# One accumulation bank for a unit's split and plain products, scaled in place, with new lists for the whole order

## The chip, the cores and the metric

The kernel runs on one core of one Trainium2 chip. The metric is the device time of one execution in microseconds; the figure given is the median of several runs. An engine is called by the short name that the profile uses: PE (TensorE, matmuls), PEld (its weight loads), DVE (VectorE), ACT (ScalarE), POOL (GpSimd), SP (SyncE, which issues most DMAs).

## The reference

The input x has 4 batches of 12416 rows of 128 channels. An attention block with 32 inducing rows comes first, then a gated feed-forward layer with RMS norm, of width 1536. Both in fp32.

```python
def mab(q, kv):
    s = scale * (q @ kv.transpose(0, 2, 1))
    s = s - s.max(-1, keepdims=True)
    a = np.exp(s)
    a /= a.sum(-1, keepdims=True) + 1e-09
    return a @ kv
h = mab(I, x)
x = mab(x, h)                       # (4 * 12416, 128)

rms = np.sqrt(np.mean(x * x, axis=-1, keepdims=True) + 1e-06)
xn = x / rms * rms_g
g = xn @ w_gate                     # 128 -> 1536
silu = g * (1.0 / (1.0 + np.exp(-g)))
out = (silu * (xn @ w_val)) @ w_out # 1536 -> 128
```

## The kernel before

**Tiling.** The rows of a batch are cut into 7 sets, and these into 25 units of 512 columns (the sixth set's are 480, the last one's 256): 100 units in all. Rows stand in columns, so a unit is a moving operand of 128 x 512. The width 1536 is cut into 12 pieces of 128; one piece of one unit is a block, 1200 in all. The list `sorts` gives each block one of three kinds.

**One block.** `gate` (L720) and `value` (L748) are one matmul each, with operands rounded to fp32r in two halves so that the sum is nearly fp32. `silu` (L730) takes the gate from PSUM on ACT. `times_value` (L762) multiplies it by the value on DVE. What follows depends on the kind:

- P, plain: the factor u is fp32 in SBUF, and `project_plain` multiplies it by the fp32 third matrix (L818, tile `wo`). The profile shows each of these fp32 products as two matmul instructions.
- S, split on DVE: u stays in PSUM. `high` (L775, ACT) rounds it to fp32r, scaled by about -2^-12; `low` (L781, DVE) makes the rest; `project_two` issues two fp32r matmuls (L806, L807); `add_in_place` (L826, POOL) adds the two parts; `project_third` issues a third fp32r matmul (L818, through `project`).
- D, split on POOL: u is in SBUF, `high` is at L772, `low_of_u` (L788) is on POOL and `high_down` (L794) on ACT; then as S.

**One unit.** The two matmuls of all its split blocks sum in one PSUM bank, `ups`. The thirds and the plain products sum in another, `acc`. `scale_up` (L850, ACT) reads `ups`, multiplies by 1 + 2^-12 and writes it to a buffer o in SBUF, four column groups apart. `finish` (L859, DVE) adds `acc` to it, `turn_out` (L865, DVE) transposes it in 32 x 32 blocks in place, `store` (L880) issues four DMAs.

**Order.** Everything is written out by hand, as lists of letters that were found beforehand: `program` is the order in which instructions are emitted, so the order on each engine; `.` in it is a step of attention, of its norm or of the preparation of weights, taken from `micros` by the list `taken`. `banks` gives the PSUM bank (of 8) for each matmul result, `holders` the buffer (of 19, 9 in pool `up` and 10 in three spare tiles of x) for u, high and low, `outputs` the buffer o, `sorts` the kinds, and `picks` which of the blocks that wait for a step is taken next. An engine takes its instructions in that order and waits at each until its operands are there.

**Around it.** The first 42 us load x, the weights and the first attention scores (`first`); after that the block loop runs to the end, with the attention of the next batch between the blocks. `rooms` runs between the two: the tiles of x of sets 2 to 4 of the first batch become the 10 further buffers.

Of the kernel before, what the change touches and what calls it, by code (L numbers as in the profile page):

```python
# [18 lines left out]
P = 128  # L19
# [4 lines left out]
def kernel(  # L24
# [40 lines left out]
    RING, HELD, SILU = 4, 9, 3  # L65
# [17 lines left out]
    psum = pool("psum", 1, space=PSUM)  # L83
    pall = psum.tile([P, 8, 512], F32, name="gv")
# [9 lines left out]
    def load_rows(b, s):  # L94

        n = per[s]
        t = xnat[b, s] = xnp.tile([P, 16 if b and n > 4 else n, C], F32, name=f"xn{s % 2 if b and n > 4 else s}")
# [592 lines left out]

    blocks, kinds = [], []
# [7 lines left out]
    def unit_of(b, u):  # L699
        if (b, u) not in at_unit:  # L700
            s, q = units[u]
            at_unit[b, u] = {"T": per2[s] * m, "a": moving.pop((b, u)), "left": NJ, "q": 0, "acc": None,
                             "k": sum(kind != "P" for kind, one in zip(kinds, blocks) if one[:2] == (b, u)), "o": None,
                             "ups": None}
# [92 lines left out]
    def project_two():  # L797
# [4 lines left out]
        if one["ups"] is None:  # L802
            one["ups"] = bank()
        to = one["ups"][:, 0:T]
# [6 lines left out]
    def project(n, lhsT, rhs, step2):  # L811
# [3 lines left out]
        if one["acc"] is None:  # L815
            one["acc"] = bank()
        to = one["acc"][:, 0:T]
        nc.tensor.matmul(to.rearrange("p (n h) -> p h n", h=2) if step2 else to, lhsT, rhs,  # L818
                         start=one["left"] == NJ, stop=one["left"] == 1)
# [18 lines left out]
    leaving = {name: 0 for name in "EFTO"}  # L838

    def next_unit(name):  # L840
        leaving[name] += 1
        return flat[leaving[name] - 1]

    def scale_up():
# [3 lines left out]
        T, o = one["T"], output(F32)  # L848
        one["o"] = o
# [11 lines left out]
    def turn_out():  # L861
        b, u = next_unit("T")
        one = unit_of(b, u)
        o, T = one["o"], one["T"]
# [393 lines left out]
    def seams():  # L1258
# [13 lines left out]
        5674130256741352764156216710562160121607267012750671527162067125701527061352701372301273016276370142374017436107  # L1272
        5461701375601735764301674317642376476324736426173214672670321071507125625625730261325620463042603435423046754672
        6571574124615247601207502765127520730717157312014520712054051402460524124361406470341720123014073145207145205162
        4076176230451603542360267402340264706402613067507602716510250673501637521352614563175416571674605740534715702545
        3457042563253265431275126142745265124560124607164701640316370347147057304132041201372013720317603270307256042750
        4756027457256347203174063021462176270675246510461307635063450634573460543604265230541265026504265026316241321643
        1064370613041320741327342735407234507234657403254130421502401325140275130732713621762170617301612506031041234610
        4621046513052135720175237120372130276215601670416415074560743514305436543215362160524062534217541646314735673157
        3561746147560274265462502530726546253601460362013460724104270371274205402507215724175061045614061306531405310463  # L1280
        5013674034130461204372104672503725074604365073047654304716046074107160721504712670235072130536725603505237062407
        2314760162062746015412574251346547516421541257642576072605210572153701357127034152342375276132436236724632174260
        7540152406524150621504361053606250125726507650216745012475627452743564527342654736024670261720742160726034704320
        1472014721542015430174301574231654215634251467354216352615236025301253012765320532154725347254712563174217637523
        0752370635767540372103120437204312072430730145703175601314341703641706327102751301341735407364103410543265123614
        2351425312634175725647256172010457015472134270321026701630513620712605763476237062046267210473623561561453612546
        3210523025043570145370641763120547163047305173501630763120750674561027475467045074507245626034013453165034150326
        4520132435743051217230723165016371043651306704754053640356435270342704175027517251427507164721453264534516342164
        5320164532405127451723407312403612753123512561726532756127032160342560324053246302542164321024052472014725041275
        4327031240370173104731643143072641362013562150613570615263174521621452643256416312654036254720764065205621562756  # L1290
        0461043103560401403507471054615042704627160734102374130415021704170527054761045260123646504615304673106351670515
        6725120513657106723017346123461762167341527647362746502364576215367425762156246276570647274635074067450367513541
        3657426517365127605360130232046352162146574051760415704761350735705327537210570673160752635725473427635274152645
        3273157425073215023576031706527106241065476140173546703573061362013651036013243162015714251640542016204310546154
        3103601765732053210642367412702173273407417520715231603573156743061471567051725417627452617425143610742642604276
        0124051264701256140
    """
    workers = """
        20120201201201020120122201201201201201211210210201020120110120120
    """  # L1300
    outputs = """
        10101010101010101010101010101010101010101010101010101010101010101010101010101010101010101010101010101010
    """
    holders = """
        abcdefghibcaedfghbicjkadelmfghnobcidepqarsfgbhidjkaeclmpnfoqrsgjhbidklaecpnfgdombrqsjihpagoecdfbknilmpghrqfsjlmc
        pkinobrsadqjhpkgfelmnoqcjrspbliadnmjkoqsglhrfejpaodnqbscriekjapmlnsqogkrbfpjhsaecokqrmdilnopgskmhqbcjrefolmnipqs
        ajdgchmkfepoirnbgqlsrpmckjfoqglnpsmibkohadprelsjmcgfnkbqolpiahdrjemsqfrcgbhnoiljepkqmrsdnloaqjifrcgpmsonblkqejrp
        hsgialnfqpojmkdsrlnqcpombeijsplqhfdagknromqepijchalskdgfbrmepqjnhgaifcokjpbrlqgeinosmdrlajpqhskmnrcfbloqmjidesag
        frklcjpqnosmhbdrlgiejkafdqpcbrmelonsfgcqjidpkhablroqenmfgicdjshaoedcinpqlgbjkhsdiorfbhgemnaqocspfjkrigbhdlmasncq
        pfedjorgbsnkclqmhefirjabposknlqemdrgibfhpoqscajnlmfhkrpecidjnbgqosljmafkdpnrqcoskihgbpefcadjlmrhosapndqkgehpjmin  # L1310
        obflrqdspkcmjnqholgaesbfkpdolhminqfjrskcpogmljdfnrqbpcaoskjhgiqmlpnefodqrmknlpcsmijknabolpshgjeidbfocgnkhqrplmjs
        oaifehgcnbdkpqclhrgfdesmjnrofkqilpgsrobkdjqlmhcnseljamrpqknfoiglspmcoqjkldhrsnpelabjmokqngircjfdhblsemqpnokjgamq
        rdlipejfmscpqonklhmgsaberjocpikmlpdsrhefqngobaljpikdmhcqsrleonfagbmpjreqolciknmpsqholfjgbakderichfsnmqopaljbrkcf
        moglhiaedbrjckqegdpsnlfrjiedkqmoaghcpsnrfblmikendagojlqhcfbmpiarsnlgckmfdhqbpoidejnaqkhipdgerbasohjlgmqienpfkrcs
        adhjnglmbpsqofekrjpidgscbljqnhepkafomgisqrnbplkcohjmfsrgkpaqbeoijdlsgnmqrfeokabpjnmlcgqhafdibeopgsrklnjcqmobkgln
        hsqdpriomajlkceshnpbofiarqsmndgejklobipnhcsgldefmraqchbjkopaslmnqirohjgdqbpmeknfsalrcidjfqokegplsdjmrknbsphcgljr
        mqasifnpeokljdhcgfrqmsolnpbekjromialsfnqpkgrjmondqlhscpnkrmbefiaojsqglkdphnmrclskoerigapjnrfbkdhlosqnmpkrsjelgpi
        acnhfjrmlpoqkdnsjbremgqkfjapdhnrifmlcesqjkbgophnrmjceoslpnadkqimofjgnbshdrlcminjoeafbkqdgpschmnjofrpdksblqamrige
        jnchpoblkqsfdagmjirnpohecqslkrpbmjdfnloqaskighmoeqcbsjrpnlagqmdikshofnejcabrlgqpdmkohirnbsldfaqjcpmkoriegsqlknjp
        ofdbshemrlqpncsgoaibklpmejshnqorkcjbplnfksqomjrdgapnqkoemicrlphjqbgnmorsfakjploqcsdnipebghorfcqksmlpjonradbcqfse  # L1320
# [240 lines left out]
```

## Time and profile before

| | |
|---|---|
| Median of 3 runs | 1467.7 us (1467.61 to 1468.09) |
| Span of the profiled execution | 1467.1 us |
| What lies around the span | 0.6 us from the span to the median |
| Instructions in the profile | 25864 |
| HBM | 53.95 MB read, 27.00 MB written |

The profile is one execution. Its span goes from the first to the last instruction. "Busy" is the time in which an engine has an instruction running; matmuls are pipelined, so the length of one record (0.38 us for 512 columns) is not what it takes of PE; the distance between starts is. A group's line gives its count, the busy time and the mean of one in ns, then the idle time of the engine just before such instructions and what ended it.

### The profile page before, as it was taken

The page shows a single profiled execution, that of the slowest core. Times are in us where ns is not written, and L with a number is a line of the kernel's source. Part 1 is how long each engine was busy: PE and PEld are TensorE (multiplying, and loading weights), DVE is VectorE, ACT ScalarE, POOL GpSimd, SP SyncE. Part 2 cuts the span into 40 slices and gives each one's busy share as a digit, 9 for nine tenths or more (in the row PEclk, how much of TensorE's full clock was granted, in tenths as well). Part 3 has the DMA queues.
Part 4 walks back from the last instruction along what each step waited for, and adds up shares of the span by engine and source line. Part 5 has one row for each costly group of instructions (what it writes and reads, how often), then busy time and mean ns, then how long its engine had stood idle before and what let it go on. Part 6 is the DMA issues. An engine that isn't in the chain of part 4 may idle for free.

```text
span 1467.1 us, 25864 instructions
## 1 busy us (share of the span) xinstructions
PE 1460.2 (100%) x7293; PEld 1111.8 (76%) x7293; DVE 1423.3 (97%) x2476; ACT 1300.0 (89%) x2586; POOL 1353.0 (92%) x1193
## 2 busy tenths in 40 slices
PE   9999999999999999999999999999999999999998
PEld 7556777877777777786777778777778778788787
DVE  6999999999999999999999999999999999999998
ACT  6798899889988989988999899888998999899987
POOL 2578998999999999899999999799999999999998
PEclk9999999999999999999999999999999999999999
DMA  7656224445654222635554132355123111222121
GB/s 282 137 99 119 58 49 92 103 107 99 118 88 99 38 44 44 141 84 105 110 101 82 26 73 43 63 119 127 34 62 70 33 37 39 43 42 38 36 45 33
DMA packets 391904, 116.02 MB, mean 79 GB/s; under 512 B 365648, under 2 KB 371280, under 8 KB 389200
## 3 DMA queue, kind: packets, MB, share of 16 engines
q1 hardware_dynamic: 391168, 114.28, 37.7%
q8 instruction: 58, 0.95, 0.3%
q14 instruction: 86, 0.70, 0.2%
q10 hardware_dynamic: 592, 0.08, 0.0%
HBM read 53.95 MB, written 27.00 MB: 55 GB/s over the span
## 4 chain that ended last, share of the span: by engine, by line
PE 99%; DVE 0%; DMA 0%; ACT 0%; issue 0%; DVEq 0%
PE gv L818 33%; PE gv L720 17%; PE gv L748 17%; PE gv L806 12%; PE gv L807 12%; PE gv L327 3%; PE gv L380 1%; PE gv L945 1%; PE gv L574 1%; PE gv L989 0%; PE gv L468 0%; PE gv L158 0%; PE gv L490 0%; DMA ind<-in_inducing_dram 0%; PE gv L567 0%; PE gv L1099 0%
## 5 line engine op out<-in xcount | busy, mean ns | idle before, releaser
L730 ACT ACTIVATE silu<-gv 128x512 f32<-128x512 f32 (+2 forms) x1200 | 678.1, 591 | 89.4 <-PE gv L720 67.4
L826 POOL TENSOR_TENSOR xn<-xn,xn 128x512 fp32r<-128x512 f32 (+2 forms) x363 | 453.0, 1259 | 23.4 <-PE gv L807 14.5
L720 PE MATMUL gv<-a,sg 128*128 128x512 f32 (+2 forms) x1188 | 463.5, 415 | 0.1
L748 PE MATMUL gv<-a,sv 128*128 128x512 f32 (+2 forms) x1188 | 460.9, 415 | 0.0
L762 DVE TENSOR_TENSOR gv<-silu,gv 128x512 f32<-128x512 f32 (+2 forms) x649 | 427.1, 673 | 6.5 <-ACT silu L730 2.2
L775 ACT ACTIVATE xn<-gv 128x512 fp32r<-128x512 f32 (+2 forms) x602 | 353.1, 594 | 25.8 <-DVE gv L762 20.5
L818 PE MATMUL gv<-u,wo 128*128 128x512 f32 (+2 forms) x742 | 364.1, 576 | 0.0
L762 DVE TENSOR_TENSOR u<-silu,gv 128x512 f32<-128x512 f32 (+2 forms) x551 | 352.3, 654 | 7.8 <-PE gv L748 3.7
L826 POOL TENSOR_TENSOR u<-xn,u 128x512 fp32r<-128x512 f32 (+2 forms) x239 | 298.3, 1257 | 5.6 <-PE gv L807 4.1
L720 PEld LDWEIGHTS gv<-a,sg 128*128 128x128 f32 x1188 | 223.9, 189 | 86.8 <-issue 21.5
L748 PEld LDWEIGHTS gv<-a,sv 128*128 128x128 f32 x1188 | 223.8, 189 | 80.6 <-issue 23.0
L781 DVE SCALAR_TENSOR_TENSOR xn<-xn,gv 128x512 fp32r<-128x512 f32 (+2 forms) x410 | 268.9, 662 | 4.7 <-ACT xn L775 2.7
L826 POOL TENSOR_TENSOR xn<-xn 128x512 fp32r<-128x512 f32 (+2 forms) x170 | 211.4, 1250 | 11.4 <-PE gv L807 10.3
L806 PE MATMUL gv<-xn,xn 128*128 128x512 f32 (+2 forms) x450 | 177.4, 394 | 0.0
L818 PEld LDWEIGHTS gv<-u,wo 128*128 128x128 f32 x742 | 139.1, 190 | 29.7 <-issue 14.2
L788 POOL TENSOR_TENSOR xn<-u,xn 128x512 fp32r<-128x512 f32 (+2 forms) x123 | 152.3, 1243 | 6.8 <-ACT xn L772 5.5
L781 DVE SCALAR_TENSOR_TENSOR u<-xn,gv 128x512 fp32r<-128x512 f32 (+2 forms) x192 | 125.8, 660 | 1.2 <-ACT xn L775 0.9
L818 PE MATMUL gv<-xn,xn 128*128 128x512 f32 (+2 forms) x299 | 117.3, 398 | 0.0
L806 PE MATMUL gv<-xn,more 128*128 128x512 f32 (+2 forms) x302 | 116.0, 385 | 0.0
L794 ACT ACTIVATE xn<-xn 128x512 fp32r<-128x512 f32 (+2 forms) x170 | 105.6, 623 | 8.2 <-POOL xn L788 4.0
L807 PE MATMUL gv<-xn,xn 128*128 128x512 f32 (+2 forms) x299 | 111.6, 373 | 0.0
L772 ACT ACTIVATE xn<-u 128x512 fp32r<-128x512 f32 (+2 forms) x170 | 104.9, 621 | 3.9 <-DVE u L762 1.7
(233 smaller groups left out, 2049.8 us busy)
## 6 DMA issues: line engine op xcount, KB each, us to landing
out_dram<-o SPq DMA_DIRECT2D x320, 64.0 KB, 2.0
xT<-in_x_dram SPq DMA_DIRECT2D x60, 256.0 KB, 4.1
xn<-in_x_dram SPq DMA_DIRECT2D x60, 256.0 KB, 5.0
a<-hi SPq DMA_DIRECT2D x152, 64.0 KB, 2.0
a<-lo SPq DMA_DIRECT2D x152, 64.0 KB, 2.0
xn<-in_x_dram SPq DMA_DIRECT2D x5, 1024.0 KB, 9.6
xn<-w SPq DMA_DIRECT2D x18, 256.0 KB, 4.6
out_dram<-o SPq DMA_DIRECT2D x64, 60.0 KB, 2.1
```

Of the source, the lines that this page charges most:

```text
L720: nc.tensor.matmul(g[:, 0:T], stacks[b][0][:, ts(j, P)], halves_in_turn(one["a"][:, 0:T]), start=True, stop=True)
L730: nc.scalar.activation(sl[:, 0:T], gates.pop(n)[:, 0:T], AF.Silu)
L748: nc.tensor.matmul(v[:, 0:T], stacks[b][1][:, ts(j, P)], halves_in_turn(one["a"][:, 0:T]), start=True, stop=True)
L762: nc.vector.tensor_tensor(out=to, in0=sl[:, 0:T], in1=v[:, 0:T], op=ALU.mult)
L775: nc.scalar.activation(hi, t["u"], AF.Copy, scale=-(1.0 - 2.0 ** -13) * 2.0 ** -12)
L781: nc.vector.scalar_tensor_tensor(out=t["lo"], in0=t["hi"].bitcast(F32), scalar=4096.0, in1=t["u"], op0=ALU.mult, op1=ALU.add)
L788: nc.gpsimd.tensor_tensor(out=t["lo"], in0=t["u"], in1=t["hi"].bitcast(F32), op=ALU.subtract)
L794: nc.scalar.activation(t["hi"], t["hi"].bitcast(F32), AF.Copy, scale=-(2.0 ** -12))
L806: nc.tensor.matmul(to, weight_of(0, j), halves_in_turn(t["hi"]), start=not one["q"], stop=False)
L807: nc.tensor.matmul(to, weight_of(1, j), halves_in_turn(t["lo"]), start=False, stop=last)
L818: nc.tensor.matmul(to.rearrange("p (n h) -> p h n", h=2) if step2 else to, lhsT, rhs, start=one["left"] == NJ, stop=one["left"] == 1)
L826: nc.gpsimd.tensor_tensor(out=t["lo"], in0=t["hi"].bitcast(F32), in1=t["lo"].bitcast(F32), op=ALU.add)
```

## The change

In all units but the first four (`APART = 4`), `project_two` sums into the same bank as the thirds and plain products, `acc`. When a unit's last second matmul is done, `scale_up` multiplies that bank by 1 + 2^-12 in place, PSUM to PSUM, and only then the thirds and plain products of the unit are added to it (`start` is false for them). `finish` is left out for these units. `turn_out` transposes from PSUM, through the strided view that `finish` and `scale_up` used, into o. E, T and O, which took units in turn, now take them by `picks`.

The 10 further buffers are tiles of a pool of their own, `ring`, each with a name, in the room of another pool, `xlp`, that holds sets 2 to 4 of the first batch and is closed in `rooms`; before they were slices of three tiles.

All lists are new. The counts that can be read from them:

| list | before | after |
|---|---|---|
| `sorts`: P, S, D | 371, 649, 180 | 338, 718, 144 |
| `program`: F | 100 | 4 |
| `program`: h, q, d, r each | 829 | 862 |
| `program`: l, n and e, p | 649, 180, 371 | 718, 144, 338 |
| `program`: g, s, v, m, and E, T, O | 1200 each, and 100 each | the same |
| `banks` | 2707 | 2611 |
| steps in `taken` | 879 | 879, the same ones in another order |

The lists of the first 42 us (`BANKS`, `WORKERS`, `OUTPUTS`, `ORDER`) are unchanged.

```diff
+    late = {"ctx": ctx.enter_context(ExitStack())}
+    late["x"] = late["ctx"].enter_context(tc.tile_pool(name="xlp", bufs=1))
...
     def rooms():
         kws["first"] = xnp.tile([P, half + NK, C], F32R, name=f"xn{full - 1}")
-        rings = [xnp.tile([P, RING * 512], F32R, name=f"xn{full - 4 + n}") for n in range(3)]
-        for n in range(3 * RING - 2):
-            kws[HELD + n] = rings[n // RING][:, ts(n % RING, 512)]
-        kws["last"] = rings[2][:, 2 * 512:4 * 512].rearrange("p (k c) -> p k c", c=C)
+        late["ctx"].close()
+        late["ring"] = pool("ring", 1)
+        kws["last"] = late["ring"].tile([P, 8, C], F32R, name="last")
...
     def room(kind=F32R):
         n = factors.pop(0)
-        return up.tile([P, 512], kind, name="u", tag=f"u{n}") if n < HELD else kws[n]
+        return (up if n < HELD else late["ring"]).tile([P, 512], kind, name="u", tag=f"u{n}")
...
     def project_two():
...
-        if one["ups"] is None:
-            one["ups"] = bank()
-        to = one["ups"][:, 0:T]
+        name = "ups" if one["apart"] else "acc"
+        if one[name] is None:
+            one[name] = bank()
+        to = one[name][:, 0:T]
...
     def project(n, lhsT, rhs, step2):
...
+        assert one["apart"] or one["scaled"]
         to = one["acc"][:, 0:T]
         nc.tensor.matmul(to.rearrange("p (n h) -> p h n", h=2) if step2 else to, lhsT, rhs,
-                         start=one["left"] == NJ, stop=one["left"] == 1)
+                         start=one["apart"] and one["left"] == NJ, stop=one["left"] == 1,
+                         skip_group_check=not one["apart"])
...
-    leaving = {name: 0 for name in "EFTO"}
+    leaving = {name: flat[:APART] if name == "F" else list(flat) for name in "EFTO"}
     def next_unit(name):
-        leaving[name] += 1
-        return flat[leaving[name] - 1]
+        return leaving[name].pop(choices.pop(0))
     def scale_up():
...
+        if not one["apart"]:
+            one["scaled"], to = True, one["acc"][:, 0:T]
+            nc.scalar.activation(to, to, AF.Copy, scale=1.0 + 2.0 ** -12)
+            return
...
     def turn_out():
...
+        if not one["apart"]:
+            assert not one["left"]
+            o = one["o"] = output(F32)
+            nc.vector.transpose(out=o[:, 0:T].rearrange("p (q n) -> p q n", q=R), in_=in_order(one["acc"][:, 0:T]))
+            return
```

More of the change, by code (lines that the diff above doesn't have):

```diff
@@ L64 @@
     NK = NJ - 2
-    RING, HELD, SILU = 4, 9, 3
+    HELD, SILU = 9, 3
+    LATE = range(full - 4, full - 1)
     def pool(name, bufs, **kw):
@@ L96, in load_rows @@
         n = per[s]
-        t = xnat[b, s] = xnp.tile([P, 16 if b and n > 4 else n, C], F32, name=f"xn{s % 2 if b and n > 4 else s}")
+        of_set = late["x"] if not b and s in LATE else xnp
+        t = xnat[b, s] = of_set.tile([P, 16 if b and n > 4 else n, C], F32, name=f"xn{s % 2 if b and n > 4 else s}")
         if b or s == full:
@@ L701, in unit_of @@
             s, q = units[u]
-            at_unit[b, u] = {"T": per2[s] * m, "a": moving.pop((b, u)), "left": NJ, "q": 0, "acc": None,
+            at_unit[b, u] = {"T": per2[s] * m, "a": moving.pop((b, u)), "left": NJ, "q": 0, "acc": None, "scaled": False,
                              "k": sum(kind != "P" for kind, one in zip(kinds, blocks) if one[:2] == (b, u)), "o": None,
-                             "ups": None}
+                             "ups": None, "apart": flat.index((b, u)) < APART}
         return at_unit[b, u]
@@ L847, in scale_up @@
         assert one["k"] and one["q"] == one["k"]
-        T, o = one["T"], output(F32)
-        one["o"] = o
+        T = one["T"]
+        if not one["apart"]:
[3 more added lines that the diff above has]
+        o = one["o"] = output(F32)
         nc.scalar.activation(o[:, 0:T].rearrange("p (q n) -> p q n", q=R), in_order(one["ups"][:, 0:T]), AF.Copy,
@@ L863, in turn_out @@
         one = unit_of(b, u)
-        o, T = one["o"], one["T"]
+        T = one["T"]
+        if not one["apart"]:
+            assert not one["left"]
+            o = one["o"] = output(F32)
+            nc.vector.transpose(out=o[:, 0:T].rearrange("p (q n) -> p q n", q=R), in_=in_order(one["acc"][:, 0:T]))
+            return
+        o = one["o"]
         nc.vector.transpose(out=o[:, 0:T], in_=o[:, 0:T])
@@ L1276 @@
[L1276 to L1280, printed above, removed]
@@ L1296 @@
-        0124051264701256140
+        0123456701345607134561732563457643754375643765463547635472653742657462564276452367543265346753264756410524710526
+        7026571206752137652137626726312573672374563275430430256403547065340634710710376015031546150463521042306142056407
+        6347154067043674170417507645071256470126472057120464324531046315632564126310635026351206152706173023605721640571
+        4516241745106275307130627156207165230621273613562457215714732573156372316735607257035170367106501647034513453147
@@ new lines @@
+        5061754734075175312075130457421734103271402673123160326471364231672436752315673427135273421340537541543502412304
+        3524130261306215643260340213640310712604123476262164273647536174263712534213641536043203542634652613245613724563
+        2167531452165314263012015326124615402560451470615420601720572605176025372036271032516502516034126012543162312563
+        0215261073261305170213762103671234172034167032142701372415032137423754057051240756472506725146751427614526427562
+        34524162341536423145612450643645032
@@ new lines @@
+        vdmsqrvlhdsvqgrgmlmhsqvrhlmlmdagqvpehshsvqqgqlddmlsqTmgdddqvsmgvgEvrrvgssmmhgrmlshlvprrgvrmhshshdmlldngvpqshmvgv
+        sqgmmlqgdrvssqrgqrhmldddgvqrhOOalehss.lmdqqdvgsqvggddTEmgvsphmhmllvrrrrrvmsdshgshqgvmrq.rvpvlmlmhhsdlgqgvndhmrgq
+        vrlsvsmsedmhmlqggvgqsmvqdgsmshsdvqgmvEpvdddsrrrhgmlhmllqprrgqvTshhslddmgvshmlqgvshdlmlqpgdgvvsmmqvqrgshaOdlgvqrr
+        hslmddvqsmgsmvqgpvEvrgrshmhmlhslgplsmrgddTshvqqvgmlvqvgsrgsmsmqrgrmphddhdhsdlqllggvvqvrvqmdsEsmOmOrpdrrprpTmprrp
+        rrpdprTOO
```

380 lines of the change are left out of this document (188 added, 192 removed), and 62 rows, old and new, of the table taken.

## The prediction

> **What bounds the kernel now.** I read the page's busy times first, then the stages, then the groups kept apart by shape, and last the order of time around single events.
>
> ```profile
> PE 1460.2 (100%) x7293; PEld 1111.8 (76%) x7293; DVE 1423.3 (97%) x2476; ACT 1300.0 (89%) x2586; POOL 1353.0 (92%) x1193
> PE 99%; DVE 0%; DMA 0%; ACT 0%; issue 0%; DVEq 0%
> ```
> ```profile
> 42.00:1462.00 1420.00, 1419.92 (x6829) 1080.09 (x6828) 1392.61 (x2382) 1274.01 (x2526) 1341.73 (x1166) 1.00 0.37 73
> 1462.00:1467.00 5.00, 0.12 (x2) 0.00 (x0) 0.87 (x2) 0.00 (x0) 0.00 (x0) 0.76 0.35 55
> ```
>
> From 42 us to 1462 us PE is busy for 1419.92 of 1420 us at a granted clock of 1.00, and the chain of waits is 99% PE. A busy PE alone proves little, because matmul ends are modelled. So I look at the distance from one start to the next.
>
> ```profile
> 903.07 0.38 PE L807 MATMUL gv<-u,xn 128*128 128x512 f32 x1
> 903.28 0.38 PE L818 MATMUL gv<-u,xn 128*128 128x512 f32 x1
> 903.48 0.60 ACT L850 ACTIVATE o<-gv 128x512 f32<-128x512 f32 x1 [0.21 <-PE gv L807]
> 903.50 0.38 PE L748 MATMUL gv<-a,sv 128*128 128x512 f32 x1
> 903.71 1.02 PE L818 MATMUL gv<-u,wo 128*128 128x512 f32 x2
> 904.14 0.19 PEld L720 LDWEIGHTS gv<-a,sg 128*128 128x128 f32 x1 [0.24 <-ACT o L850]
> 904.17 0.78 PE L720 MATMUL gv<-a,sg 128*128 128x512 f32 x1
> 904.79 0.38 PE L748 MATMUL gv<-a,sv 128*128 128x512 f32 x1
> ```
>
> An fp32r matmul over 512 columns takes a slot of 0.216 us (903.07, 903.28, 903.50). A plain fp32 product is two instructions: from 903.50 to 904.79 stand one value, one plain and one gate, 1.29 us, so the plain one costs 1.29 - 2 x 0.216 = 0.858 us. Take these slots, 1200 gates, 1200 values, 829 split blocks of three matmuls and 371 plain blocks, with the narrower units in proportion to their width: 1333 us. Laid end to end against the recorded starts, stretch by stretch, they leave no idle time that exceeds the rounding of the slots. PE does not wait for anybody in the block loop; the time is PE's own work, and only less work on PE, or new waits of PE, can move it.
>
> **The change part by part.** Counting letters of the list of block kinds in the diff: plain blocks (P) 371 to 338, blocks split on DVE (S) 649 to 718, blocks split on POOL (D) 180 to 144. The other lists keep 1200 gates, silus, values and products.
>
> PE. A plain block costs 0.858 us in the third matrix product, a split one 3 x 0.216 = 0.648: 0.210 us less for each. Of the 33 conversions 25 are 512 wide, 3 are 480 and 5 are 256: 25 x 0.210 + 3 x 0.197 + 5 x 0.105 = 6.4 us less. All of it lies on the path, since PE never waits.
>
> The other engines, by these rows:
>
> ```profile
> L762 DVE TENSOR_TENSOR gv<-silu,gv 128x512 f32<-128x512 f32 x539 | 361.3, 686 | 4.2 <-PE gv L748 1.8 <-ACT silu L730 0.5 <-ACT o L850 0.2
> L762 DVE TENSOR_TENSOR u<-silu,gv 128x512 f32<-128x512 f32 x421 | 278.2, 674 | 6.4 <-PE gv L748 3.4 <-ACT silu L730 1.8
> L781 DVE SCALAR_TENSOR_TENSOR xn<-xn,gv 128x512 fp32r<-128x512 f32 x332 | 221.5, 675 | 3.5 <-ACT xn L775 1.6 <-POOL xn L826 0.3 <-issue 0.2
> L826 POOL TENSOR_TENSOR xn<-xn,xn 128x512 fp32r<-128x512 f32 x286 | 364.4, 1285 | 21.3 <-PE gv L807 12.9 <-DVE u L762 4.4 <-ACT xn L775 1.4
> L788 POOL TENSOR_TENSOR xn<-u,xn 128x512 fp32r<-128x512 f32 x95 | 121.4, 1283 | 5.7 <-ACT xn L772 4.8 <-ACT xn L595 0.3
> L775 ACT ACTIVATE xn<-gv 128x512 fp32r<-128x512 f32 x500 | 298.3, 604 | 19.8 <-DVE gv L762 15.6 <-PE gv L720 0.7 <-PE gv L818 0.4
> L794 ACT ACTIVATE xn<-xn 128x512 fp32r<-128x512 f32 x135 | 86.0, 639 | 7.3 <-POOL xn L788 3.5 <-POOL u L788 2.9
> L850 ACT ACTIVATE o<-gv 128x512 f32<-128x512 f32 x80 | 48.3, 604 | 3.1 <-PE gv L807 2.7
> L859 DVE TENSOR_TENSOR o<-gv,o 128x512 f32<-128x512 f32 x80 | 54.3, 679 | 2.6 <-PE gv L818 1.9 <-issue 0.4 <-ACT o L850 0.2
> L865 DVE STREAM_TRANSPOSE o<-o 128x512 f32<-128x512 f32 x80 | 55.9, 698 | 0.1
> L441 DVE STREAM_TRANSPOSE sc<-gv 128x512 f32<-128x512 f32 x19 | 12.8, 691 | 0.7 <-PE gv L327 0.6
> ```
>
> DVE loses 96 additions of 0.679 us (76 of 512, 16 of 480, 4 of 256: 63.6 us) and gains 69 lows of S blocks (50, 13 and 6 of the three widths at 0.675 us: 44.6 us) and 69 x 0.012 us because an S product goes to PSUM (0.8 us): 18 us less. POOL loses 36 subtractions of 1.283 us and gains 33 additions of 1.285 us, narrow ones in proportion: about 5 us less. ACT gains 33 highs of 0.604 us and loses 36 of 0.639 us: about 4 us less. None of this is on the path; it widens the cover of PE, with DVE at 1405 of some 1461 us.
>
> The transpose now reads PSUM, and with a stride. From PSUM without a stride it takes 691 ns (L441), and the addition L859, which reads the same strided view of the bank, takes 679 ns beside 674 ns for L762: both bounds are within 12 ns of the 698 ns of today, and I take 698.
>
> [...]
>
> Scaling in place. Before, the first matmuls of a unit's split blocks summed in one bank, and the third and plain products in another, so nobody on PE waited for the scaling. Now the chain is last second-matmul, scaling on ACT, first third or plain product, all on one bank. Behind the waiting product stand all later matmuls of PE, and behind them every engine. Its length: ACT starts 0.41 us after the start of the matmul (903.07 to 903.48), 0.20 after its slot; the scaling takes 0.604 us; then PE.
>
> ```profile
> 1090.65 1.69 ACT L730 ACTIVATE silu<-gv 128x480 f32<-128x480 f32 x3
> 1091.26 0.19 PEld L720 LDWEIGHTS gv<-a,sg 128*128 128x128 f32 x1 [0.45 <-ACT silu L730]
> 1091.27 0.47 PE L720 MATMUL gv<-a,sg 128*128 128x480 f32 x1
> 1091.57 0.37 PE L806 MATMUL gv<-xn,xn 128*128 128x480 f32 x1
> ```
>
> This is one of the few places where PE waits for ACT today: the first of three silus (0.563 us each) ends at 1091.21, the weights start at 1091.26, and the next matmul comes 0.30 us after L720 instead of 0.20. So PE resumes 0.05 + 0.10 = 0.15 us after ACT's end. The turn takes 0.20 + 0.604 + 0.15 = 0.96 us. What covers it is PE work that the list puts between: in the order of the program list, counted for the 96 units and left out attention's own matmuls, the median is 1.08 us, five matmuls; only three units have less than 1.0 us and no attention step beside it, with 0.86, 0.86 and 0.96 us. So the usual unit has 0.12 us to spare, and the three cost 0.2 us together.
>
> What ACT needs in place, PSUM to PSUM, no row shows. Lower bound: 604 ns (L850, L775). Upper bound: 639 ns (L794, the slowest source) plus 12 ns (L762 into PSUM against SBUF), 651 ns. Both fit in the 0.12 us. I take 604, the same reader and source.
>
> [...]
>
> Lateness. The list of before is in the order of starts. Beside the trace, nine in ten scalings of line 850 start at most 0.10 us after the matmul that stands next in the list, and 98 of 100 at most 0.33 us after. If the new list holds as well, one unit in ten is about 0.1 us over its spare and two in a hundred 0.2: 0.015 us a unit, 1.4 us in 96. With the three above I take 1.6 us.
>
> Banks and buffers. From its first sum to its last reader a unit held 12 + 15 us of bank time in PE's clock, now 20, so seven fewer; no row shows PE waiting for a bank. But all thirds and plain products of a unit now come after all its firsts, so factors live longer: walking both lists, 12 of the 19 buffers are full on average before (at most 18) and 15.6 after (at most 19). That is taken at nothing, covered by DVE's 18 us, and is a rival below. The pool that closes for the ring's buffers held sets 2 to 4, whose readers all stand before the block loop: nothing.
>
> The tail.
>
> ```profile
> 1461.73 0.39 PE L818 MATMUL gv<-u,more 128*128 128x256 f32 x2
> 1462.21 0.42 DVE L859 TENSOR_TENSOR o<-gv,o 128x256 f32<-128x256 f32 x1 [1.42 <-PE gv L818]
> 1462.67 0.45 DVE L865 STREAM_TRANSPOSE o<-o 128x256 f32<-128x256 f32 x1
> 1463.14 1.54 ACTq L880 DMA_DIRECT2D out_dram<-o  x2
> ```
>
> The addition after the last matmul goes: 1462.67 - 1462.21 = 0.46 us, 0.4 taken.
>
> Sum: 1467.1 (span) - 6.4 - 0.4 + 1.6 = 1461.9. The median of the runs, 1467.7, lies 0.6 above the span: **1462.5 us**.
>
> **The rivals.** (1) **ACT comes late to the scaling; slower.** ACT is in order and 89% busy. If the list did not place the scaling, ACT would be inside another instruction with a chance of 0.89 and have 0 to 0.604 us to go; beyond 0.12 us spare that is 0.89 x 0.484 x 0.484 / (2 x 0.604) = 0.17 us a unit, 16.6 us in all: 1467.7 - 6.8 + 16.6 = 1477.5. It decides from 6.8 / 96 = 0.07 us a unit. For it: today the scaling found ACT waiting only 6 times in 100 (the row of L850, 2.7 us to PE). Against it: today nothing hung on it, and starts follow the list to 0.1 us.
>
> (2) **Buffers take the gain back; no change.** With 19 of 19 full, a product of DVE waits for a third on PE, its low comes late, and PE misses a slot of 0.216 us. Once in three units this is 32 x 0.216 = 6.9 us: 1467.7 - 6.8 + 6.9 = 1467.8. For it: 15.6 against 12 buffers. Against it: DVE has 18 us more room, and the shortest distances on PE between a gate and the use of its factor hardly change (5% are under 4.45 us before, under 4.32 after).
>
> (3) **The scaling in place is slow**, say twice a pass: 0.604 - 0.12 = 0.48 us x 96 = 46 us, 1507. Against it: L762 reads and writes the same bank in place in 686 ns, beside 674 to SBUF.
>
> (4) **The lists do not do what they say**: PE's order is the same length but the tail or the attention stretches between the blocks (1467 - 42 - 1333 - 5 = 87 us) lose a slot or two at each of 14 sets and pieces: 28 x 0.216 = 6 us, 1467.
>
> **How the numbers follow.** The forecast has 0.55, with its own range 1459.5 (no lateness, and 1.5 us out of the attention stretches) to 1466.5 (5.6 us of lateness in place of 1.6). Rival 1 has 0.20, 2 has 0.17, 3 has 0.03, 4 has 0.05. A measurement of this kernel tells about 0.2%, 2.9 us, from no change. Faster: 0.51 of the forecast's 0.55 and 0.03 of rival 2, 0.54. Same: 0.03 of the forecast, 0.03 of rival 1, 0.10 of 2 and 0.04 of 4, 0.20. Slower: the rest, 0.26. The range reaches from 1459.8 up to 1475, most of rival 1.
>
> **What would show it.** Right: L818 with wo 66 records fewer, distances of 0.216 in the loop, the wait of PE's third product for ACT's scaling under 3 us in sum, DVE near 1405 us. Rival 1: weights of L818's successor waiting for ACT at the scaling line, 10 us or more. Rival 2: DVE's product waiting for PE's third. Rival 3: the scaling over 0.72 us. I am wrong if PE's idle time in the loop passes 4 us, or if PE's work does not fall by 6 us.

## The result and the profile after

| | before | after |
|---|---|---|
| Median | 1467.9 us (1467.6 to 1468.7, 4 runs) | 1481.3 us (1479.8 to 1482.5, 4 runs) |
| Span of the profiled execution | 1467.1 us | 1480.8 us |

The kernel got slower by 13.4 us: the ratio is 1.0089, with a 95% interval of 1.0075 to 1.0103. The forecast of 1462.5 us was wrong in size and in sign, and the time lies above the range. The profiled execution of the kernel after is its longest, 1482.5 us.

The page of the kernel after, with the busy times and the shares of the chain that ended last:

```profile
PE 1470.6 (99%) x7326; PEld 1107.9 (75%) x7326; DVE 1412.3 (95%) x2449; ACT 1296.2 (88%) x2587; POOL 1347.2 (91%) x1190
PE 96%; DVE 1%; SPq 1%; DMA 1%; POOL 0%; ACT 0%; issue 0%; DVEq 0%; POOLq 0%; ACTq 0%
```

DVE, ACT and POOL all have less to do, as forecast. PE is still 99% busy and still the chain. So the loss lies on PE, in a form that a busy time doesn't show. The removed work is really gone: in the groups of both pages, here the plain third product of before and then of after,

```profile
L818 PE MATMUL gv<-u,wo 128*128 128x512 f32 (+2 forms) x742 | 364.1, 576 | 0.0
```
```profile
L824 PE MATMUL gv<-u,wo 128*128 128x512 f32 (+2 forms) x676 | 335.0, 580 | 0.0
```

66 records are missing, 33 blocks of two. The idle time that the profile puts down to waits of PE in the kernel after is small too (the three largest; columns: who waited for whom, us in total, times, longest):

```profile
PE gv L724 <- DVE u L766: 1.7, 1, 1.7
PE gv L162 <- POOL ident masks.py:199: 1.3, 1, 1.3
PE gv L724 <- DVE sg L501: 1.0, 1, 1.0
```

So I split PE's time by the distances between the starts of its matmuls. Every matmul of the block loop gets the slot of the prediction (0.216 us, plain 0.429 per record, narrower ones in proportion). What a chain of loop matmuls takes beyond its slots is "excess". A stretch of matmuls that are not of the loop (attention, norm, weights) is measured from the loop matmul before it to the second one behind it, less two slots; where a single loop matmul stands between two stretches, the two are measured as one, so that nothing counts twice. "Tiled runs" hold what PE computes in tiles of 128 x 32 or 32 x 32 over up to 512 columns: the sets of scores (L331, before L327; eight matmuls each), the stacks of weights (L472, before L468) and the squares for the norm (L578 and L571, before L574 and L567). Two of these are in one run when no loop matmul stands between them. (Two runs of each kernel are squares over the full array. The sums of h, L384, are tiled too, over 128 columns; they stand in 9 runs and take 19.8 us in both kernels.)

| us | before | after | change |
|---|---|---|---|
| first loop matmul | 42.7 | 41.8 | -0.9 |
| slots of the loop | 1332.1 | 1325.7 | -6.4 |
| excess in the loop | -0.3 | 7.9 | +8.2 |
| attention and the like on PE | 87.5 | 100.3 | +12.8 |
| of it in tiled runs | 60.6 in 27 runs | 74.4 in 60 runs | +13.8 |
| after the last slot | 5.2 | 5.1 | -0.1 |

But for rounding, the parts add up to the spans and to their difference, +13.7. The attention computes the same as before with the same instructions, and takes 12.8 us more of PE. One place of this is a wait that the traces of experiments 4, 6, 7 and 8 don't have: at 738 us the squares wait for a DMA (start, length, what; from the chain of work), and the stretch takes 2.51 us there, 1.36 to 1.37 in those four.

```profile
735.03 4.56 DMA xn<-xn
739.64 1.05 PE gv L578 x6
```

Without it the growth is 11.6 us, 12.6 in the tiled runs. What differs is where they stand. Before, in the order of time on PE (start, length of the record, line, tile, shape, number):

```profile
306.01 0.38 PE L720 MATMUL gv<-a,sg 128*128 128x512 f32 x1
306.32 1.06 PE L327 MATMUL gv<-xT,hT 128*32 128x512 f32 x8
307.20 0.60 PE L468 MATMUL gv<-xn,hg 128*32 128x512 f32 x3
...
311.91 1.42 PE L327 MATMUL gv<-xT,hT 128*32 128x512 f32 x7
313.26 0.70 PE L720 MATMUL gv<-a,sg 128*128 128x512 f32 x2
313.80 0.38 PE L806 MATMUL gv<-xn,xn 128*128 128x512 f32 x1
```

After, the same stage:

```profile
304.25 0.38 PE L724 MATMUL gv<-a,sg 128*128 128x512 f32 x1
304.56 1.06 PE L331 MATMUL gv<-xT,hT 128*32 128x512 f32 x8
305.56 0.48 PE L752 MATMUL gv<-a,sv 128*128 128x512 f32 x1
305.97 1.06 PE L331 MATMUL gv<-xT,hT 128*32 128x512 f32 x8
...
315.60 0.38 PE L752 MATMUL gv<-a,sv 128*128 128x512 f32 x1
315.91 1.07 PE L331 MATMUL gv<-xT,hT 128*32 128x512 f32 x8
316.90 0.48 PE L824 MATMUL gv<-u,xn 128*128 128x512 f32 x1
317.23 0.38 PE L724 MATMUL gv<-a,sg 128*128 128x512 f32 x1
```

Before, eight pieces (six sets of eight matmuls, two stacks of six) are one run. From the gate ahead of it to the matmul of L806 behind it are 7.79 us; less three slots of the loop, 7.14 us, 0.89 a piece. After, each set shown stands alone: from 315.60 to 317.23 are 1.63 us, less two slots 1.20 us. If entering and leaving a run costs p, eight pieces save seven: 8 x 1.20 - 7p = 7.14, so p is about 0.35 us (a stack and a narrower set taken as a set). One sees where it lies: the first tiled matmul starts 0.31 us after the full one ahead of it, not 0.216; the second full one behind comes 0.33 us after the first (316.90, 317.23); the rest, some 0.14 us, lies between the last tiled one and the first full one (eight at 0.106 us, as (2.05 - 1.20) / 8 of experiment 8, would end at 316.76). 33 more runs at 0.35 us are 11.5 us.

It is the tiles that are paid for, and not the change from fp32r to plain fp32. A piece of the attention in fp32 over the full array, here of the kernel after, costs no more than its work:

```profile
302.73 0.38 PE L752 MATMUL gv<-a,sv 128*128 128x512 f32 x1
302.95 0.38 PE L419 MATMUL gv<-fold,hl 128*128 128x128 f32 x2
303.09 0.46 PE L811 MATMUL gv<-u,xn 128*128 128x512 f32 x1
303.39 0.38 PE L812 MATMUL gv<-u,xn 128*128 128x512 f32 x1
```

From 302.73 to 303.39, less two slots, are 0.23 us, against 2 x 0.429 x 128 / 512 = 0.21. The squares over the full array at 293.6 us of the kernel before (L567, two records of 480 columns) take 0.80 us, the two slots of plain records of that width.

The groups by shape don't show this. The scores of before and of after:

```profile
L327 PE MATMUL gv<-xT,hT 128*32 128x512 f32 x152 | 24.2, 598 | 0.0
```
```profile
L331 PE MATMUL gv<-xT,hT 128*32 128x512 f32 x152 | 20.2, 604 | 0.0
```

The busy time of this group fell and one record is as long as before; the price lies in the distances to the neighbours.

The rows price the way into tiles and out of them at 0.35 us; what PE does in that time they don't show.

The 8.2 us more of excess have two large single places. The first ends at 1133.6 us (order of time, all engines; SPq is SP issuing DMAs):

```profile
1121.03 2.18 SPq L896 DMA_DIRECT2D out_dram<-o  x4
1123.25 1.78 SPq L489 DMA_DIRECT2D sv<-whi  x3
1125.08 2.22 SPq L896 DMA_DIRECT2D out_dram<-o  x4
1127.34 1.78 SPq L489 DMA_DIRECT2D sv<-whi  x3
1129.17 1.86 SPq L489 DMA_DIRECT2D sv<-wlo  x3
```
```profile
1132.54 0.71 DVE L636 STREAM_TRANSPOSE aT<-sc 128x512 f32<-128x512 f32 x1 [2.78 <-DMA sv<-wlo]
1133.18 0.38 DVE L766 TENSOR_TENSOR u<-silu,gv 128x256 f32<-128x256 f32 x1
1133.61 0.38 PE L724 MATMUL gv<-a,sg 128*128 128x256 f32 x1 [1.67 <-DVE u L766]
```

SP issues 17 DMAs in 10 us, two units' stores ahead of and between three groups of weights' DMAs. A transpose on DVE waits 2.78 us for the last of these, the product behind it comes late, and PE's next gate stands still for 1.67 us. Around this place the loop loses 4.1 us. Not all of it is waiting: from 1134.25 to 1137.66 us the granted clock is 0.5 in this trace, and slots take twice as long (0.41 us from 1135.38 to 1135.79, for an fp32r matmul of 480 columns that takes 0.20 elsewhere). In the traces of experiments 4 and 8 the gate waits as long, 1.8 us, the clock stays at 1.00, and the place costs 2.7 us. So the profiled execution of after has some 2.6 us that those two don't have, 1.15 of the DMA at 738 us and 1.4 of the clock; the fastest run of after is 2.7 us shorter than the profiled one. The second place is at 68 us: DVE waits for POOL (L1100), the subtraction L501 behind it comes late, and a gate waits 1.0 us; some 1.2 us are lost.

The scaling in place, the step that the prediction was most concerned with: its group, the transpose from PSUM and the other transpose from PSUM, then what the view of line 857 says of its waits.

```profile
L857 ACT ACTIVATE gv<-gv 128x512 f32<-128x512 f32 x76 | 44.7, 589 | 19.2 <-PE gv L812 18.3
L878 DVE STREAM_TRANSPOSE o<-gv 128x512 f32<-128x512 f32 x76 | 53.4, 702 | 0.1
L445 DVE STREAM_TRANSPOSE sc<-gv 128x512 f32<-128x512 f32 x19 | 13.3, 702 | 0.8 <-PE gv L331 0.8
```
```profile
  PE gv L812: 23.4, 33
who waited for it (us, times):
  PEld gv L752: 1.1, 2
  PEld gv L724: 0.8, 1
  PEld gv L331: 0.3, 1
  DVE u L766: 0.3, 1
  PEld gv L824: 0.2, 1
```

In 33 of 96 units the profile lists ACT as idle ahead of the scaling, until the second product, 23.4 us in sum; in the other 63 it lists no such wait. PE's weights waited for the scaling 2.4 us in five places (0.2 us of it the third product). The instruction takes 589 ns, 15 less than the lower bound that was taken.

### The profile page after: what moved, and what is told of

Its sections match the earlier page's. It is cut to its first block, busy times and chain, and to the rows that moved or that the text cites. A ratio compares the mean times of both kernels' runs of the same rounds, so it can differ in the third digit from the quotient of the medians.

```text
span 1480.8 us, 25956 instructions
## 1 busy us (share of the span) xinstructions
PE 1470.6 (99%) x7326; PEld 1107.9 (75%) x7326; DVE 1412.3 (95%) x2449; ACT 1296.2 (88%) x2587; POOL 1347.2 (91%) x1190
## 4 chain that ended last, share of the span: by engine, by line
PE 96%; DVE 1%; SPq 1%; DMA 1%; POOL 0%; ACT 0%; issue 0%; DVEq 0%; POOLq 0%; ACTq 0%
PE gv L824 30%; PE gv L752 17%; PE gv L724 17%; PE gv L811 12%; PE gv L812 12%; PE gv L331 3%; PE gv L384 1%; PE gv L961 1%; PE gv L578 1%; PE gv L162 0%; DMA xn<-xn 0%; PE gv L472 0%; PE gv L1005 0%; SPq L489 0%; DVE u L766 0%
## 5 line engine op out<-in xcount | busy, mean ns | idle before, releaser
L833 POOL TENSOR_TENSOR u<-u 128x512 fp32r<-128x512 f32 (+2 forms) x862 | 1051.7, 1250 | 47.8 <-PE gv L812 39.9
L766 DVE TENSOR_TENSOR gv<-silu,gv 128x512 f32<-128x512 f32 (+2 forms) x718 | 466.7, 671 | 10.3 <-PE gv L752 4.8
L785 DVE SCALAR_TENSOR_TENSOR u<-u,gv 128x512 fp32r<-128x512 f32 (+2 forms) x718 | 460.4, 660 | 15.6 <-ACT u L779 12.5
L779 ACT ACTIVATE u<-gv 128x512 fp32r<-128x512 f32 (+2 forms) x718 | 414.4, 597 | 27.4 <-DVE gv L766 19.6
L824 PE MATMUL gv<-u,wo 128*128 128x512 f32 (+2 forms) x676 | 335.0, 580 | 0.0
L766 DVE TENSOR_TENSOR u<-silu,gv 128x512 f32<-128x512 f32 (+2 forms) x482 | 309.6, 656 | 14.8 <-PE gv L752 6.1
L792 POOL TENSOR_TENSOR u<-u 128x512 fp32r<-128x512 f32 (+2 forms) x144 | 178.2, 1244 | 14.4 <-ACT u L776 6.7
L824 PE MATMUL gv<-u,more 128*128 128x512 f32 (+2 forms) x396 | 158.7, 415 | 0.0
L811 PE MATMUL gv<-u,more 128*128 128x512 f32 (+2 forms) x396 | 155.9, 394 | 0.0
L812 PE MATMUL gv<-u,more 128*128 128x512 f32 (+2 forms) x396 | 147.7, 373 | 0.0
L811 PE MATMUL gv<-u,xn 128*128 128x512 f32 (+2 forms) x323 | 128.8, 399 | 0.0
L824 PE MATMUL gv<-u,xn 128*128 128x512 f32 (+2 forms) x323 | 125.2, 405 | 0.1
L812 PE MATMUL gv<-u,xn 128*128 128x512 f32 (+2 forms) x323 | 120.3, 373 | 0.0
L824 PEld LDWEIGHTS gv<-u,more 128*128 128x128 f32 x396 | 75.0, 190 | 27.1 <-issue 14.4
L776 ACT ACTIVATE u<-u 128x512 fp32r<-128x512 f32 (+2 forms) x144 | 89.3, 624 | 3.3 <-PE gv L824 1.5
L798 ACT ACTIVATE u<-u 128x512 fp32r<-128x512 f32 (+2 forms) x144 | 89.4, 625 | 1.9 <-POOL u L792 1.9
```

Of the source, the lines that this page charges most:

```text
L766: nc.vector.tensor_tensor(out=to, in0=sl[:, 0:T], in1=v[:, 0:T], op=ALU.mult)
L779: nc.scalar.activation(hi, t["u"], AF.Copy, scale=-(1.0 - 2.0 ** -13) * 2.0 ** -12)
L785: nc.vector.scalar_tensor_tensor(out=t["lo"], in0=t["hi"].bitcast(F32), scalar=4096.0, in1=t["u"], op0=ALU.mult, op1=ALU.add)
L792: nc.gpsimd.tensor_tensor(out=t["lo"], in0=t["u"], in1=t["hi"].bitcast(F32), op=ALU.subtract)
L798: nc.scalar.activation(t["hi"], t["hi"].bitcast(F32), AF.Copy, scale=-(2.0 ** -12))
L811: nc.tensor.matmul(to, weight_of(0, j), halves_in_turn(t["hi"]), start=not one["q"], stop=False)
```

## The experiments

The theory: PE pays for every change between the full array and tiles, and the new lists change 33 more times (60 runs in place of 27). Its rivals: the scaling in place, with the lateness that it brings; single waits that the new order makes; or something in the new block order as such that has nothing to do with tiles.

**1. and 2. Every set for itself, in both kernels.** A small full-array matmul stands ahead of each set and each stack of the block loop, so that no two share a run. It writes 32 columns of the bank that the set then starts anew.

```diff
+    def apart_from_last(ps):
+        if flowing:
+            nc.tensor.matmul(ps[:, 0:32], ident[:], ident[:, 0:32], start=True, stop=True)
...
             ps = bank()
+            apart_from_last(ps)
```

Before with it:

> The kernel before, with one small full-array fp32 matmul (32 columns, into the bank that the set is about to overwrite) ahead of each of the 54 attention sets in the block loop (48 score sets, 6 stacks). It adds 54 small matmuls and splits about 34 places where two sets stood side by side on PE. Fragment theory (PE loses about 0.335 us each time it goes from the block loop to a set that is tiled by columns and back): 34 x 0.335 = 11 us on top of the 54 matmuls alone, which the kernel after, with the same matmuls, prices. Wait theory (the loss of the changed kernel is waits on late operands and DMAs): only the 54 matmuls, some 3 to 8 us, the same in both kernels.

After with it:

> The changed kernel with the same 54 small matmuls. Only about 5 sets stand side by side on PE here, so by the fragment theory it costs the 54 matmuls and 5 x 0.335 = 2 us, some 9 us less than the same edit costs the kernel before; by the wait theory both cost the same.

Measured: 1487.1 us from before (ratio 1.0131, 1.0114 to 1.0148) and 1489.5 from after (1.0149, 1.0134 to 1.0164). The same edit costs before 19.2 us and after 8.2 us. Of the gap of 13.4 us between the two kernels 2.4 us are left once no set or stack directly follows another tiled piece in either. The small matmul is plain fp32 over the full array, so it is again the change of tiles that costs. The lists of before hold 34 sets and stacks that directly follow another tiled piece, those of after 4: 11.0 us over 30 are 0.37 us each. By the distances on PE the attention with the small matmuls is 106.4 us in before and 108.1 in after.

**3. The sets of after put back together.** Only the lists of the kernel after are changed: sets are moved to stand beside others, 42 runs in place of 60, with banks given anew.

```diff
     taken = """
-        ... 301 302 288 303 311 310 292 293 308 ...
+        ... 301 288 302 292 303 293 311 310 308 ...
```

> The changed kernel with nothing but the order of attention sets on PE edited: sets are moved next to each other, with their readers on DVE where needed and with new banks, so that runs of sets between blocks fall from 58 to 42 (before: 28). Fragment theory: 16 x 0.335 = 5.4 us less, about 1476. Wait theory: no gain, or a loss where a bank is now tighter, 1481 or more.

Measured: 1513.6 us (1.0309, 1.0294 to 1.0324), a miss. The stretches of attention took 108.6 us, more than the 100.3 ahead of the edit, and the loop's excess rose from 7.9 to 30.0 us; the granted clock is 0.5 for 13.7 us in three places of this trace, which is about 7 us of it. Two lines of its waits of PE:

```profile
PE gv L724 <- DVE wlo L482: 5.2, 3, 3.1
PE gv L472 <- DMA xn<-w: 2.4, 1, 2.4
```

The second line is a stack that waits for the weights it reads; the first is gates that wait behind the stacks' readers on DVE. So this run says nothing of the price; it says that sets can't be put together afterwards at no cost in lists in which all else has its place.

**4. The scaling left out.** The kernel after without the scaling in place of its 96 units.

```diff
-            one["scaled"], to = True, one["acc"][:, 0:T]
-            nc.scalar.activation(to, to, AF.Copy, scale=1.0 + 2.0 ** -12)
+            one["scaled"] = True
```

> The changed kernel without the scaling in place of the 96 units (the factor 1 + 2^-12 on the split part is left out), so no product of a unit waits for ACT. By the trace of the changed kernel PE waits 0.2 us for that line in sum: under 1.5 us of change, 1480 to 1482. If ACT's lateness were the loss (the first rival of the prediction): about 16 us less, 1465.

Measured: 1478.8 us (1.0076, 1.0061 to 1.0091), 2.5 us less than after, where under 1.5 was expected; the 16 us of the first rival are refuted. The size is loose, because the runs of the two kernels overlap (1478.6 to 1480.8 here, 1479.8 to 1482.5 of after) and because the trace of after has 2.6 us that this one hasn't. Experiment 7 against 6 is the cleaner pair, 1.9 us. All of the chain second product, scaling, third product, its lateness and ACT's share, is thus worth some 2 us. The attention keeps 99.0 us, that of after less the wait for the DMA.

**5. The sets of before scattered.** The counterpart: the kernel before with all its instructions, where single matmuls of the loop (gates, values, thirds, plain products) are moved by some places to stand between two sets; 56 runs in place of 27. The first of these moves, in the list of letters (p is a plain product):

```diff
     program = """
-        ..s.v.v.g.mgp.s...v.p.m.sm.vg.g..sgaps.vm...mh..m.l...
+        ..s.v.v.g.mgp.s...v..m.sm.vg.g..sgas.vm...mh.p.m.lp...
```

> The kernel before with the same instructions; only 29 matmul steps of the block loop (thirds, plain products, gates, values) are moved on PE by at most some 30 list places, each in between two attention sets that stood side by side, so that the runs of sets grow from 27 to 56. Fragment theory: 29 x 0.335 = 9.7 us slower (11 by the pair of kernels with small matmuls, 0.38 each), 1477 to 1479, and the stretches of attention on PE grow by that while the block loop does not. Wait theory: no more than 2 us, 1468 to 1470.

Measured: 1480.1 us (1.0084, 1.0069 to 1.0099), 12.4 us slower than before and a little more than was forecast, nearly as slow as the kernel after, with none of the change in it. The excess rises by 2.4 us only; the attention takes 97.2 us in place of 87.5. In the stage shown above:

```profile
307.21 0.38 PE L720 MATMUL gv<-a,sg 128*128 128x512 f32 x1
307.52 1.07 PE L327 MATMUL gv<-xT,hT 128*32 128x512 f32 x8
308.52 0.48 PE L818 MATMUL gv<-u,xn 128*128 128x512 f32 x1
308.93 1.06 PE L468 MATMUL gv<-xn,hg 128*32 128x512 f32 x6
```

These are the distances of the kernel after (0.31, 1.00, 0.41). 9.7 us over 29 runs are 0.33 us each; by the time, 12.4 - 2.4 = 10.0 over 29 are 0.34.

**6. The two places of waiting.** The kernel after with the three DMAs of weights issued ahead of the two units' stores, and the subtraction L501 ahead of the transpose that waits for POOL. Steps 536, 535, 537 and 58 of the attention are moved:

```diff
     taken = """
-        ... 46 56 57 47 64 67 48 58 32 ...
-        ... 811 552 814 812 815 ... 833 830 834 536 535 537 858 ...
+        ... 46 56 57 58 47 64 67 48 32 ...
+        ... 811 552 536 535 537 814 812 815 ... 833 830 834 858 ...
```

> The changed kernel with four steps moved: three of the issues that spread a batch's second stack (nine DMAs on SP's queue) from behind two stores to ahead of them, and the subtraction that ends the last gate stack ahead of the transpose that waits for POOL. Queue theory: PE's gaps at 1131 to 1138 us and at 68 us, 4.0 and 1.2 us of idle beyond the matmul slots, go, 1476; the stretches of attention stay at 101 us. If these gaps only hide a lateness that comes out elsewhere: 1480 to 1482.

Measured: 1477.9 us (1.0069, 1.0052 to 1.0085), 3.5 us less than after, where 5.2 were expected by the queue theory, and below the 1480 to 1482 of its rival. Neither of the two places is among the waits of PE any more; but for two of the first 42 us, 1.3 and 0.4 us, there are two of 0.2 us. The excess is 3.2 us, and the clock stays at 1.00. The runs now lie within 0.3 us (1477.7 to 1478.1), where those of after spread over 2.7.

**7. Both.** Experiments 4 and 6 in one kernel.

> Both: the four steps moved, and the scaling in place of the 96 units left out. If the parts add up, 5 + 2.5 us less than the changed kernel, 1474, the block loop on PE with less than 2 us beyond its slots, and what is left above 1461 (the kernel before less 6.4 and 0.4 us) is the attention stretches' 13 us. If ACT's scaling and the queue hide each other: 1476 or more.

Measured: 1476.0 us (1.0055, 1.0040 to 1.0070), 5.3 us less than after; 7.5 was expected if the parts add up, and 1476 or more if they hide each other. Of the parts as measured, 2.5 and 3.5, it is most. The excess is down to 2.0 us and the profile shows one wait of PE in the loop, 0.3 us for a DMA, yet the time is still 8.3 us above before, although 6.4 us of slots are gone. The attention takes 99.0 us against 87.5 before: 11.5 us, 12.6 in the tiled runs, 0.38 for each of the 33 more. With 2.3 us of excess over before's, 6.4 us of slots gone and a loop that begins 0.3 us earlier, that is the 7.1 us between the two spans. The other 1.2 us are not in the change: the span of before that is profiled, 1467.1 us, is 1.2 us longer than its typical one in the runs beside this experiment, 1465.9 us for a time of 1467.7. (So 1.8 us lie around a span, not the 0.6 of the table; the forecast is a difference to the median and doesn't hang on it.)

**8. Some sets of after joined, where that is near.** As experiment 3, but a set or what stands between two is moved by a few places only; 55 runs in place of 60.

> The kernel after, with single sets of scores moved by some places in its lists to stand beside another set, where a bank was free: 55 runs of tiled matmuls on PE instead of 60, everything else in the order of after. If entering a run of tiled matmuls costs PE 0.34 to 0.39 us, it is 1.7 to 2.0 us faster than after (1481.3), 1479.3 to 1479.6, and the attention stretches fall from 101.1 to about 99.3 us; a moved set may make one wait of its own, which would show as excess of the block loop above 7.1 us. If the number of runs is not what costs (what the attention computes is unchanged), the time stays at 1481.3 and the stretches at 101.1.

Measured: 1483.0 us (1.0099, 1.0082 to 1.0116), a miss in the time. The attention did fall, from 100.3 to 98.2 us, but 1.15 us of this is the wait for the DMA at 738 us, which this execution doesn't have. The five joins are worth 0.8 us together, less than half of what was expected. One of them, the two single sets shown of after, gives the full price:

```profile
305.98 0.38 PE L752 MATMUL gv<-a,sv 128*128 128x512 f32 x1
306.29 1.92 PE L331 MATMUL gv<-xT,hT 128*32 128x512 f32 x16
308.14 0.48 PE L811 MATMUL gv<-u,more 128*128 128x512 f32 x1
308.46 0.38 PE L812 MATMUL gv<-u,more 128*128 128x512 f32 x1
```

From 305.98 to 308.46 are 2.48 us, less two slots 2.05, against 2 x 1.20 = 2.40: 0.35 us, as above. The other four give less, and one of them, at 198 us, nothing; why is open. And new waits came, this one of 0.7 us and another of 0.6:

```profile
PE gv L752 <- ACT silu L734: 0.7, 1, 0.7
```

The excess rose by 1.0 us, and in the profiled execution the loop began 1.3 us later, in a stretch that the edit doesn't touch. The span, 1481.0 us, is that of after to 0.2 us, and the runs of the two kernels overlap (1479.8 to 1482.5 of after, 1481.5 to 1483.5 here). So the trace shows in one place what a join can be worth, and neither the time nor the sum over the five confirms it.

## Why the prediction was wrong

**What failed.** The step that failed is the sentence that "only less work on PE, or new waits of PE, can move it", and with it a term that the sum doesn't have. The prediction counted every list for the kinds of blocks, the scaling and the buffers, and took the attention's 87 us on PE as they were, because its instructions didn't change. The same work in another order cost some 11.5 us more of PE without a wait. Only rival 4 put a loss there, "a slot or two at each of 14 sets and pieces", 6 us at a chance of 0.05. The place was right; the unit was wrong. What is paid is not a slot per set but about 0.35 us each time PE goes from the full array to tiles and back, and that happens 33 more times. Both figures could be had beforehand: the number of runs from the two orders of PE, the price from the trace of before, where an isolated set and sets side by side both stand. The line of the table of lists that looked harmless, "the same ones in another order", was the change that decided.

How sure is the size? The price of a run is 0.35 us in single places of two kernels, 0.37 by experiments 1 and 2, 0.33 to 0.34 by experiment 5, and 0.38 by the tiled runs of experiment 7 against before. 33 runs are then 11 to 12.5 us. Joining five runs in experiment 8 gave back 0.2 us a run only, so the price is shown for scattering (experiments 1, 2 and 5), and not for mending.

**Point by point.**

- PE sets the end, and 33 conversions save 6.4 us: right, 6.4 us of slots and 66 records fewer, outweighed three times over by the rest.
- Relief of the others: right in sign. DVE is 11 us less busy, not 18, though its instructions as summed one by one fall by 16 (1599 to 1583 us): records that overlap count once in a busy time. POOL 6, not 5; ACT 4. None of it showed in the time, as said.
- Transpose from PSUM with a stride: taken as 698 ns, measured 702, and the strideless L445 beside it 702 as well.
- Scaling in place: taken as 604 ns, measured 589, 15 less. ACT starts 0.42 us after the second product's start where it is free (0.41 assumed).
- Lateness: 1.6 us forecast; PE's weight loads waited 2.4 us for the scaling, and leaving it out gives 1.9 to 2.5 us (experiments 7 and 4). The term was too small by under 1 us. In 63 of 96 units the profile lists no wait of ACT ahead of the scaling, so ACT may have come late in these; that this is why is not shown.
- Rival 1 (ACT late, 16.6 us): its mechanism exists, at a seventh of its price. Its time, 1477.5, is closer to the result than the forecast's, by luck: the loss has another reason.
- Rival 2 (buffers take the gain back): not seen; with the two places of waiting mended, the profile lists no wait of PE for DVE or POOL in the loop.
- Rival 3 (scaling slow): refuted by 589 ns.
- Banks and buffers at nothing: no run speaks against it. But the steps of the attention were only counted. Their new places put three groups of weights' DMAs behind two units' stores on SP's queue, and a subtraction on DVE behind a transpose that waits for POOL: 3.5 us, which the prediction had nowhere. The signal that it named, PE's idle time in the loop above 4 us, came only half: the waits of PE that the profile lists come to 3 us there, its distances to 8.2 more than before.
- The tail: 0.1 us less, not 0.4.

**The account.** -6.4 (slots) + 11.5 (attention on PE, experiment 7) + 5.3 (scaling and the two places, experiment 7) are 10.4 us of the 13.4 us measured. The rest is the 2.3 us of excess that experiment 7 still has over before, spread over the loop and unexplained, and under 1 us between spans and medians. The gain was there, and the scattering took it nearly twice over. With the sets in an order like before's, 27 runs, and the two places mended, the sum would be about 1467.9 - 6.4 + 2.5 = 1464 us, or 1466 if the 2.3 us stay: an estimate that no run here shows; no version measured is faster than before.

## What to carry to other kernels

When an order is written anew, compare for the bounding engine not only which instructions are issued but how often it changes its manner of working, and price one change from the trace: distance from the last instruction of the one kind to the second one back, less the slots. Here a 99% busy PE lost 0.8% to this (12 of 1480 us) without a wait in the profile. Putting pieces back together afterwards didn't pay here: both attempts (experiments 3 and 8) made waits that cost more than they saved, while moving the four steps that a wait pointed at won 3.5 us (experiment 6). And compare traces as well as times: one profiled execution of the slower kernel held 2.6 us, of a DMA that came late and a halved clock, that two others didn't.

## What the hardware showed that was not expected

PE takes about 0.35 us to go from full-array fp32r matmuls to 128 x 32 tiles and back, for short and long runs alike: 1.20 us for eight tiled matmuls of 512 columns alone, 0.85 us for eight more behind them (2.05 - 1.20), 7.14 us for eight pieces. The loss lies on both sides, 0.09 us ahead and some 0.14 and 0.11 us behind, and all of it counts as busy (PE is busy for 1.63 of the 1.63 us from 315.60 us of the kernel after). A full-array fp32 piece in the same place costs no such thing (0.80 us for 0.80 of work). And stores share a queue with transfers that somebody waits for: at 1121 and 1125 us of the kernel after, SP takes 2.18 and 2.22 us for four store issues each, and these eight put 4.4 us ahead of a DMA that DVE waits for. The granted clock was 0.5 for 3.4 us after a standstill of PE of 1.7 us in the trace of after, and stayed at 1.00 after one of 1.8 us in those of experiments 4 and 8; what decides is not shown.
